# Weight pieces cut from both halves of w_in's rows, and four decay tables made before the Silu table is loaded

## The chip, the cores and the metric

One core of one Trainium2 chip runs the whole kernel as one program. The metric is the device time in microseconds: three runs of the kernel before gave 219.44, 220.36 and 220.79 us, so the median is 220.36 us. Lower is better.

## The reference

A decaying linear attention is followed by a two-layer network with a Silu between the layers. Inputs are float32: q, k and v are (4 batches, 8 heads, 768 positions, 64), lam has one decay rate a head, w_in is 512 x 2048 and w_out is 2048 x 512. The attention goes over blocks of positions with a running 64 x 64 state per head:

```
intra = (q_b @ k_b^T * lam**(i-j) for i >= j) @ v_b
inter = (q_b * lam**(i+1)) @ state
out_b = intra + inter
state = lam**block * state + (k_b * lam**(block-1-j))^T @ v_b
...
x = attention, heads side by side: 3072 tokens x 512
h = x @ w_in                      # 3072 x 2048
out = (h * sigmoid(h)) @ w_out    # 3072 x 512
```

The sum over the 2048 hidden columns in the last line may be taken in any order, as long as column f of w_in meets row f of w_out.

## The kernel before

The 3072 tokens are cut into 24 blocks (units, `u`) of 128 positions, 6 for each batch. For each unit q and k are scaled by powers of lam, turned, multiplied into scores, masked, multiplied with v, and joined with the state from the unit before; the result, turned, is `xt` in bfloat16. Units are joined in groups of one or two. For a group, `first_product` multiplies `xt` with the 16 hidden chunks of 128 columns of `w_in_bf` (L871) and applies Silu on ScalarE (L880), and `second_product` multiplies these with the 16 row chunks of `w_out_bf` (L899). All matmuls are in bfloat16.

The program is written out by a small planner: `Plan.run` keeps a list of operations with costs, dependencies, priorities and buffer rings, walks through time as it estimates it, and so fixes one order of instructions for every engine. Each engine then runs its own order, and waits for other engines by semaphores. Where the planner sees TensorE idle early on, it puts in matmuls on zeros (`warm_ps`, L977).

All input transfers are issued by SyncE in one order (`order`): q, k and v of units 0 and 1, q, k, v of unit 2, then pieces 0 and 1 of w_in, k and v of unit 3, pieces 2 to 5 of w_in, q, k and v of unit 4, pieces 6 and 7, and later units and the eight pieces of w_out. A piece of either weight is 512 KB of float32. It lands in one of 6 slots `wst` of the tile `stage`, in the layout (128 partitions, 2, 512), and one copy on VectorE (L261) casts it into `w_in_bf` or `w_out_bf`.

Piece j of w_in has `m, a = divmod(j, 2)`: rows 256 a to 256 a + 255 and columns 512 m to 512 m + 511. A partition's share is two runs of 2 KB, from two rows that lie 128 rows apart; a row of w_in is 8 KB long. Two pieces with one m feed the same four hidden chunks, so the first product of chunks 4 m to 4 m + 3 waits for pieces 2 m and 2 m + 1. Piece j of w_out is 256 rows of 2 KB that lie one behind the other.

The transfers use eight completion semaphores in turn: each transfer that SyncE issues waits until the one eight before it in the queue has landed.

ScalarE needs a function table for Ln and Exp, and another for Silu; plain copies run with either. The table for Ln and Exp is loaded at L158, `table` (L858) loads the Silu table after the first `xt`. The helper `tables` (L652) makes `lam_bwd_h`, the decay rates of a unit's halves, in four small Exp instructions (L657), and the plan has it not before 20 us. `lam_bwd_h` is first read much later, by the units from 15 on (`attention_by_halves`, L694). Since the Exps stand behind the Silu table, the program loads the Exp table again ahead of them, and the Silu table again ahead of the first Silu (L880).

Of the kernel before, what the change touches and what calls it, by code (L numbers as in the profile page):

```python
# [9 lines left out]
AF = mybir.ActivationFunctionType  # L10
# [90 lines left out]
def kernel(  # L101
# [10 lines left out]
    nc = tc.nc  # L112
# [10 lines left out]
    KO = DFF // 128  # L123
# [12 lines left out]
    plan = Plan()  # L136
# [9 lines left out]
    def sb(o, name, shape, dtype, tag=None):  # L146
        return work.tile(shape, dtype, tag=tag or name, bufs=BUFS[tag or name], name=name)

    def bank(o, name, shape, dtype):
# [5 lines left out]
        out=lam_sb,  # L155
        in_=bass.AP(tensor=lam.tensor, offset=lam.offset, ap=[[0, 128]] + list(lam.ap)),
# [17 lines left out]
        out=ident, in_=ident, compare_op=AL.not_equal, fill=1.0,  # L174
# [6 lines left out]
        out=mask, in_=mask, compare_op=AL.is_ge, fill=0.0,  # L181
# [24 lines left out]
    for hh in range(2):  # L206
        r = slice(64 * hh, 64 * hh + 64)
# [13 lines left out]
    for hh in range(2):  # L221
        r = slice(64 * hh, 64 * hh + 64)
# [4 lines left out]
    lam_bwd_h = const.tile([128, NP, 2], F32)  # L227
    w_in_bf = const.tile([128, KI, DFF], BF16)
    w_out_bf = const.tile([128, KO, DM], BF16)
    w_in_r = moe_w_in.rearrange("(ko p) f -> p ko f", p=128)  # L230
    w_out_r = moe_w_out.rearrange("(ko p) f -> p ko f", p=128)


# [14 lines left out]
    def pace(u):  # L248

        return 0.0 if u < 8 else 57.0 + 6.0 * (u - 8)  # L250
# [35 lines left out]
    for n, (kind, j) in enumerate(order):  # L286
        if kind in "KV":
            u, p = j

            def fn(o, kind=kind, u=u, p=p):  # L290
                b, blk = divmod(u, NB)
                if p == 0:
                    val[kind, u] = regs[o["slots"]["reg"]]
                for hh in range(2):
                    nc.sync.dma_start(
                        out=val[kind, u][64 * hh:64 * hh + 64, p],
                        in_=dict(K=k, V=v)[kind][b, 2 * p + hh, blk * BLK:(blk + NL) * BLK, :].rearrange(
                            "(c s) d -> s c d", c=2 * NL))
            own = load.get((kind, (u, 0)))
            load[kind, j] = prev = plan.op({"SP": 1.1}, [prev], fn, n, alloc=["reg"] if p == 0 else [], at=pace(u) - 18.0)  # L300
            load[kind, j]["own"] = own or load[kind, j]
            continue
        tag = {"k": "kf", "v": "vf", "q": "kf" if j in plain else "qf", "i": "wst", "o": "wst"}[kind]
        us = {"kf": 1.19, "vf": 1.15, "qf": 1.8, "wst": 1.36}[tag]
        if tag == "wst" and order[n - 1][0] not in "io":
            us += 1.7
        elif tag != "wst" and order[n - 1][0] in "io":
            us -= 1.0

        if kind in "kvq" and j > 9:  # L310
            us = 0.75 * us

        def fn(o, kind=kind, j=j, tag=tag):
            if kind in "io":
                t = wst[o["slots"]["wst"]]
            else:
                b, blk = divmod(j, NB)
                sl = slice(blk * BLK, (blk + 1) * BLK)
            if kind in "kvq" and tag != "qf":
                t = sb(o, kind + "f", [128, H, 64], F32, tag)  # L320
                src = dict(k=k, v=v, q=q)[kind]
                nc.sync.dma_start(out=t, in_=src[b, :, sl, :].rearrange("h s d -> s h d"))  # L322
            elif kind == "q":
                t = sb(o, "qf", [128, H, 128], F32)
                nc.sync.dma_start(
                    out=t, in_=q[b, :, blk * BLK:(blk + 2) * BLK, :].rearrange("h (p t) d -> p h (t d)", t=2))
            elif kind == "i":
                m, a = divmod(j, 2)
                nc.sync.dma_start(out=t, in_=w_in_r[:, 2 * a:2 * a + 2, m * 512:(m + 1) * 512])  # L329
            else:  # L330
                nc.sync.dma_start(out=t, in_=w_out_r[:, 2 * j:2 * j + 2, :])
            val[kind + "f", j] = t


        o = plan.op({"SP": us}, [prev], fn, n, alloc=[tag],
                    at=pace(j) - (7.0 if j < 9 else 9.0) if kind in "kvq" else 0.0)
        o["tag"] = tag
        load[kind, j] = prev = o
    at = {key: n for n, key in enumerate(order)}
# [3 lines left out]
    for kind, w, n in (("i", w_in_bf, 8), ("o", w_out_bf, 8)):  # L343
        for j in range(n):
            def fn(o, kind=kind, j=j):
                t = val[kind + "f", j]
                m, a = divmod(j, 2)
                dst = (w_in_bf[:, 2 * a:2 * a + 2, m * 512:(m + 1) * 512] if kind == "i"
                       else w_out_bf[:, 2 * j:2 * j + 2, :])
                copy(o, dst, t)  # L350
            l = load[kind, j]
            cast[kind, j] = plan.op({"DVE": 0.8, "ACT": 1.2}, [l], fn, at[kind, j], frees=[(l, "wst")])
# [4 lines left out]
    O = {}  # L357
# [292 lines left out]

        O["vz", u] = (vc, oo, dd)

    def tables(o):
        for hh in range(2):
            r = slice(64 * hh, 64 * hh + 64)
            for c in range(2):
                nc.scalar.activation(lam_bwd_h[r, :, c], log_lam[r, hh::2], AF.Exp, scale=neg_h[r, c:c + 1])  # L657
    made = plan.op({"ACT": 1.2}, [], tables, 0, at=20.0)

    def attention_by_halves(u):  # L660

        b, blk = divmod(u, NB)
        pr = at["v", u]
        first, last = blk == 0, blk == NB - 1
        lq = load["q", u]
        home = u - (u - XH) % NL
        lk, lv = ([load[kind, (home, p)] for p in range(NP)] for kind in "KV")
        own_k, own_v = lk[0], lv[0]
        late = [plan.op({"NONE": 0.0}, [lq] + lk + lv, lambda o: None, 0, after=2.0, at=pace(u))]
# [3 lines left out]
        def cleared(name, ring, deps):  # L673

            def fn(o):
                val[name, u] = ring[o["slots"][name]]
                (nc.vector if o["eng"] == "DVE" else nc.gpsimd).memset(  # L677
                    val[name, u][:, 0:2 * NP] if name == "kp" else val[name, u], 0.0)
            return plan.op({"POOL": 0.95, "DVE": 0.49}, deps + [O.get(("own", name))], fn, pr, alloc=[name])
# [6 lines left out]
        kz = [cleared("kp", kp_all, late)] if new else []  # L686
        k_own = kz[:1]
        for hh in range(2):
            def fn(o, hh=hh):
                r = slice(64 * hh, 64 * hh + 64)  # L690
                if hh == 0 and not new:
                    val["kp", u] = kp_all[o["slots"]["kp"]]
                t = val["kp", u][:, 0:2 * NP].rearrange("p (a b) (e d) -> p a b e d", b=2, e=2)
                nc.vector.tensor_tensor(  # L694
                    t[r, :, :, hh, :], val["K", home][r, :, cs],
                    lam_bwd_h[r][:, :, :, None].to_broadcast([64, NP, 2, 64]), op=AL.mult)
            kz.append(plan.op({"DVE": 0.7}, [lq, made] + lk + late + kz[-1:], fn, pr,
                              alloc=["kp"] if hh == 0 and not new else [], frees=[(own_k, "reg")] if hh and done else []))
            k_own = k_own or kz[:1]
        k_own[0]["deps"] += [O["own", "kp"]] if ("own", "kp") in O and not new else []  # L700
# [144 lines left out]
    for u in range(NU):  # L845
        n = len(plan.ops)
        (attention if u < XH else attention_by_halves)(u)
        if u >= 8:

            for o in plan.ops[n:]:  # L850
                if "PE" in o["engines"]:
                    o["after"] = 0.8
# [2 lines left out]


    G = {}
    table = plan.op({"ACT": 1.3}, [O["xt", 0]], lambda o: nc.scalar.preload_act_table(AF.Silu), 11)  # L858

    def first_product(g):  # L860
        us = groups[g]
# [151 lines left out]
```

## Time and profile before

| what | value |
|---|---|
| median of three runs | 220.36 us |
| the profiled execution, its own time | 221.07 us |
| its span, first to last instruction | 219.4 us |
| TensorE (PE) matmuls busy | 209.7 us, 96% |
| VectorE (DVE) busy | 122.1 us, 56% |
| ScalarE (ACT) busy | 111.3 us, 51% |
| GpSimd (POOL) busy | 71.7 us, 33% |
| share of the 16 DMA engines taken by SyncE's queue (q1) | 66.6%, 33.37 MB |
| matmuls on zeros (L977) | 8.0 us in 24 instructions |
| first product, L871 | 92.5 us in 896 matmuls |
| second product, L899 | 85.1 us in 368 matmuls |
| w_in transfers, issue to landing, median | 6.9 us for 512 KB |
| w_out transfers, issue to landing, median | 7.3 us for 512 KB |

The span is the time between the first and last instruction of the profiled execution. The 1.67 us between span and that execution's time lie outside the instructions. Busy matmul time is overlapped in the records, so 96% does not say that TensorE works at its peak; where it waits is read from the timeline of its instructions. The granted TensorE clock was 0.997 of full speed.

### The profile page before, as it was taken

The numbers are of one execution on the slowest core, as the hardware profiler recorded it, in microseconds if no ns is written. First come the engines' busy times: TensorE is split into PE (matmuls) and PEld (weight loads), VectorE is DVE, ScalarE is ACT, GpSimd is POOL, SyncE is SP. The second block draws the span as 40 slices with busy tenths as digits, with TensorE's granted clock in tenths as the row PEclk, the third lists the DMA queues.
The fourth block names the chain that finished last, engine by engine and source line by source line (L and its number), as shares of the span: only waits on it lengthen the run. The fifth ranks groups of instructions, "written<-read, shape, count | busy, mean of one in ns | idle before, by whom it ended". The sixth has DMA issues, their size and how long they took to land.

```text
span 219.4 us, 4993 instructions
## 1 busy us (share of the span) xinstructions
PE 209.7 (96%) x2032; PEld 150.2 (68%) x2032; DVE 122.1 (56%) x197; ACT 111.3 (51%) x197; POOL 71.7 (33%) x106
## 2 busy tenths in 40 slices
PE   4989799999999999999999999999999999999994
PEld 1756588998774557955965599758759896854453
DVE  6776566688636786535979468089676221012121
ACT  5598677995473224731953177826617663620000
POOL 8664303036004520321723373248636710000000
PEclk9999999999999999999999999999999999999998
DMA  5998999899999989999983998775985300101212
GB/s 125 240 287 234 271 240 295 208 341 409 234 245 202 314 213 208 165 192 192 228 207 96 229 225 167 156 192 150 209 193 123 71 3 0 51 33 62 96 51 96
DMA packets 104214, 39.78 MB, mean 181 GB/s; under 512 B 93696, under 2 KB 97152, under 8 KB 104192
## 3 DMA queue, kind: packets, MB, share of 16 engines
q1 hardware_dynamic: 100496, 33.37, 66.6%
q10 hardware_dynamic: 3696, 6.10, 8.0%
q8 instruction: 16, 0.26, 0.5%
q14 instruction: 6, 0.05, 0.1%
HBM read 27.27 MB, written 6.29 MB: 153 GB/s over the span
## 4 chain that ended last, share of the span: by engine, by line
PE 79%; SPq 9%; DMA 8%; DVE 1%; issue 1%; POOL 0%; ACT 0%
PE o_ps L899 34%; PE h_ps L871 34%; DMA stage<-in_moe_w_in_dram 6%; SPq L322 4%; SPq L329 4%; DMA xt<-x_sb 2%; PE st_ps L512 2%; PE o_ps L939 2%; PE x_ps L550 1%; PE x_ps L832 1%; PE x_ps L831 1%; PE st_ps L743 1%; PE d_ps L612 1%; DVE w_in_bf L261 1%; PE d_ps L768 1%
## 5 line engine op out<-in xcount | busy, mean ns | idle before, releaser
L871 PE MATMUL h_ps<-xt,w_in_bf 128*128 128x256 bf16 (+1 forms) x896 | 92.5, 257 | 1.0 <-DMA xt<-x_sb 0.4
L899 PE MATMUL o_ps<-w_out_bf,g 128*128 128x512 bf16 x368 | 85.1, 379 | 0.0
L871 PEld LDWEIGHTS <-w_in_bf 128*128 128x128 bf16 x896 | 75.0, 98 | 9.8 <-DVE w_in_bf L261 1.3
L880 ACT ACTIVATE g<-h_ps 128x512 bf16<-128x512 f32 x96 | 56.1, 596 | 27.7 <-PE h_ps L871 26.6
L264 POOL TENSOR_TENSOR Xz<-y,lam_blk 64x256 bf16<-64x256 f32 x40 | 33.3, 831 | 83.9 <-DVE y L628 51.9
L899 PEld LDWEIGHTS <-g 128*128 128x128 bf16 x368 | 34.5, 98 | 35.3
L261 DVE COPY o_sb<-o_ps 128x512 f32<-128x512 f32 (+2 forms) x25 | 16.6, 665 | 40.5 <-PE o_ps L899 38.0
L259 ACT ACTIVATE xt<-x_ps 128x512 bf16<-128x512 f32 x19 | 11.3, 594 | 28.9 <-PE x_ps L554 16.9
L521 DVE TENSOR_TENSOR st_sb<-st_ps,mask 128x512 bf16<-128x512 f32 x30 | 19.8, 686 | 6.2 <-PE st_ps L512 5.7
L264 POOL TENSOR_TENSOR Xf<-y,lam_blk 128x256 f32<-128x256 f32 x18 | 16.2, 898 | 1.4
L261 POOL CAST Xz<-y 64x256 bf16<-64x256 f32 x18 | 9.9, 550 | 18.6 <-PE x_ps L831 9.9
L694 DVE TENSOR_TENSOR kp<-stage,lam_bwd_h 64x512 bf16<-64x512 f32 x18 | 14.3, 795 | 0.9 <-DMA kTz<-kp 0.6
L749 DVE TENSOR_TENSOR st_sb<-st_ps,mask_h 128x512 bf16<-128x512 f32 x9 | 6.2, 688 | 14.2 <-PE st_ps L743 14.2
L512 PE MATMUL st_ps<-qT,kTz 128*128 128x128 bf16 x120 | 10.9, 225 | 1.3 <-ACT kTz L259 0.8
L259 ACT ACTIVATE o_sb<-o_ps 128x128 f32<-128x128 f32 x1 | 0.3, 278 | 23.1 <-DVE o_sb L261 23.1
L512 PEld LDWEIGHTS <-kTz 128*128 128x128 bf16 x120 | 8.4, 101 | 4.5 <-ACT kTz L259 1.3
L628 DVE TENSOR_TENSOR y<-d_ps,Xf 64x256 f32<-64x256 f32 (+1 forms) x17 | 7.2, 421 | 5.4 <-PE d_ps L612 3.8
L259 ACT ACTIVATE vz<-stage 64x512 bf16<-64x512 f32 x15 | 9.4, 626 | 1.1 <-DVE vz L677 0.9
L261 DVE CAST w_in_bf<-stage 128x1024 bf16<-128x1024 f32 x8 | 6.1, 759 | 6.7 <-DMA stage<-in_moe_w_in_dram 6.7
L259 ACT ACTIVATE kTz<-tr_ps 64x512 bf16<-64x512 bf16 (+1 forms) x11 | 8.2, 746 | 2.3 <-PE tr_ps L464 2.2
L977 PE MATMUL warm_ps<-zeros 128*128 128x512 bf16 x24 | 8.0, 452 | 1.3 <-DVE pos L166 1.3
L704 DVE TENSOR_TENSOR kp<-qf,lam_fwd 128x512 bf16<-128x512 f32 x9 | 6.9, 768 | 3.5 <-DMA qf<-in_q_dram 3.3
(91 smaller groups left out, 193.3 us busy)
## 6 DMA issues: line engine op xcount, KB each, us to landing
qf<-in_q_dram SPq DMA_DIRECT2D x18, 256.0 KB, 4.1
out_dram<-o_sb ACTq DMA_DIRECT2D x17, 256.0 KB, 2.4
stage<-in_moe_w_in_dram SPq DMA_DIRECT2D x8, 512.0 KB, 6.9
stage<-in_moe_w_out_dram SPq DMA_DIRECT2D x8, 512.0 KB, 7.3
kf<-in_k_dram SPq DMA_DIRECT2D x15, 256.0 KB, 5.5
vf<-in_v_dram SPq DMA_DIRECT2D x15, 256.0 KB, 5.1
stage<-in_k_dram SPq DMA_DIRECT2D x24, 96.0 KB, 3.0
stage<-in_v_dram SPq DMA_DIRECT2D x24, 96.0 KB, 2.8
```

The source lines that it names most:

```text
L259: nc.scalar.activation(dst, src, AF.Copy)
L261: (nc.vector if o["eng"] == "DVE" else nc.gpsimd).tensor_copy(dst, src)
L264: (nc.vector if o["eng"] == "DVE" else nc.gpsimd).tensor_tensor(dst, a, b, op=op)
L322: nc.sync.dma_start(out=t, in_=src[b, :, sl, :].rearrange("h s d -> s h d"))
L329: nc.sync.dma_start(out=t, in_=w_in_r[:, 2 * a:2 * a + 2, m * 512:(m + 1) * 512])
L512: nc.tensor.matmul(val["st", u, half][:, i, :], lhsT=val["kTz", u][:, h // 2, h % 2, :], rhs=qT(h // 2), start=True, stop=True)
L521: nc.vector.tensor_tensor(val["st_sb", u, half], val["st", u, half], m[:, None, :].to_broadcast([128, 4, BLK]), op=AL.mult)
L694: nc.vector.tensor_tensor(t[r, :, :, hh, :], val["K", home][r, :, cs], lam_bwd_h[r][:, :, :, None].to_broadcast([64, NP, 2, 64]), op=AL.mult)
L871: nc.tensor.matmul(t[:, j, :], lhsT=w_in_bf[:, ko, (m * per + j) * 128:(m * per + j + 1) * 128], rhs=xts[g][:, :, ko, :] if turned(us[0]) ...
L880: nc.scalar.activation(t, val["h", g, m], AF.Silu)
L899: nc.tensor.matmul(val["o", u], lhsT=val["g", g, ko][:, i * BLK:(i + 1) * BLK], rhs=w_out_bf[:, ko, :], start=(ko == 0), stop=(ko == KO - 1))
L977: nc.tensor.matmul(t, lhsT=zeros[:, 0:128], rhs=zeros, start=True, stop=True)
```

## The change

Three edits go together.

1. A row of w_in is seen as two halves (e) of 1024 columns. Piece j now takes columns 256 m to 256 m + 255 of either half, for the same 256 rows. The piece is still 512 KB and lands in the same slot, but is issued as two transfers, one for each 128 rows; a partition's share of one transfer is two runs of 1 KB that lie 4 KB apart. Hidden chunks 4 m and 4 m + 1 now come from the first half, and chunks 4 m + 2 and 4 m + 3 from the second.
2. Piece j of w_out takes the rows that match: from row chunk 8 (j mod 2) + 2 (j div 2). It is still 256 rows in one transfer with runs of 2 KB.
3. The four Exps for `lam_bwd_h` become four operations with a priority and an earliest planned time of 6.5 us, and `table` depends on them, so they stand ahead of the Silu table on ScalarE.

```diff
-    w_in_r = moe_w_in.rearrange("(ko p) f -> p ko f", p=128)
+    w_in_r = moe_w_in.rearrange("(ko p) (e f) -> p ko e f", p=128, e=2)
...
                 m, a = divmod(j, 2)
-                nc.sync.dma_start(out=t, in_=w_in_r[:, 2 * a:2 * a + 2, m * 512:(m + 1) * 512])
+                for kk in range(2):
+                    nc.sync.dma_start(
+                        out=t[:, kk].rearrange("p (e f) -> p e f", e=2),
+                        in_=w_in_r[:, 2 * a + kk, :, m * 256:(m + 1) * 256])
             else:
-                nc.sync.dma_start(out=t, in_=w_out_r[:, 2 * j:2 * j + 2, :])
+
+                r = KO // 2 * (j % 2) + 2 * (j // 2)
+                nc.sync.dma_start(out=t, in_=w_out_r[:, r:r + 2, :])
...
-    def tables(o):
-        for hh in range(2):
-            r = slice(64 * hh, 64 * hh + 64)
-            for c in range(2):
+    made = []
+    for hh in range(2):
+        for c in range(2):
+            def fn(o, hh=hh, c=c):
+                r = slice(64 * hh, 64 * hh + 64)
                 nc.scalar.activation(lam_bwd_h[r, :, c], log_lam[r, hh::2], AF.Exp, scale=neg_h[r, c:c + 1])
-    made = plan.op({"ACT": 1.2}, [], tables, 0, at=20.0)
+            made.append(plan.op({"ACT": 0.3}, [], fn, 10.5, at=6.5))
...
-            kz.append(plan.op({"DVE": 0.7}, [lq, made] + lk + late + kz[-1:], fn, pr,
+            kz.append(plan.op({"DVE": 0.7}, [lq] + made + lk + late + kz[-1:], fn, pr,
...
-    table = plan.op({"ACT": 1.3}, [O["xt", 0]], lambda o: nc.scalar.preload_act_table(AF.Silu), 11)
+    table = plan.op({"ACT": 1.3}, [O["xt", 0]] + made, lambda o: nc.scalar.preload_act_table(AF.Silu), 11)
```

In the resulting program the order of the other engines moves little. SyncE issues the same transfers in the same order, with sixteen for w_in in place of eight. ScalarE has the four Exps two by two on either side of the first `y` copy, only one load of the Silu table, and, further on, the copy `vz` of unit 3 ahead of the copy `xt` of unit 2, where they stood the other way round. TensorE has the state product of unit 3 (L608) ahead of the second part of the first product of group 0, and VectorE the addition `y` that follows from it (L628) ahead of the cast of piece 2. GpSimd's order is the same.

## Prediction

> **What bounds the kernel now.** The 40 slices of the page come first. PE is busy in tenths 9 from the eighth slice (38 us) on, and the slices before it are mixed while the DMA engines are full.
>
> ```profile
> PE   4989799999999999999999999999999999999994
> DMA  5998999899999989999983998775985300101212
> ```
>
> So the end is where PE's packed stretch starts, plus its work. What can move the end is whatever holds PE before it is packed. The sums by stretch put the place between 23.5 and 26.4 us (columns: PE, PEld, DVE, ACT, POOL busy, granted clock, DMA share, GB/s): PE is busy 1.65 of 2.90 us there and 4.92 of 5.00 in the next stretch, at full granted clock.
>
> ```profile
> 23.50:26.40 2.90, 1.65 (x16) 0.83 (x14) 1.17 (x2) 1.93 (x4) 2.07 (x3) 1.00 0.90 247
> 26.40:31.40 5.00, 4.92 (x58) 4.27 (x59) 3.21 (x6) 2.99 (x5) 0.00 (x0) 1.00 0.99 276
> ```
>
> The timelines of PE, DVE and ACT name the two waits in it.
>
> ```profile
> 24.50 0.62 PE L512 MATMUL st_ps<-qT,kTz 128*128 128x128 bf16 x8 [0.85 <-ACT kTz L259]
> ...
> 25.61 0.38 PE L871 MATMUL h_ps<-xt,w_in_bf 128*128 128x256 bf16 x2
> 26.33 1.70 PE L871 MATMUL h_ps<-xt,w_in_bf 128*128 128x256 bf16 x14 [0.35 <-DVE w_in_bf L261]
> ```
> ```profile
> 22.30 0.69 DVE L261 CAST w_in_bf<-stage 128x1024 bf16<-128x1024 f32 x1 [1.42 <-DMA stage<-in_moe_w_in_dram]
> ...
> 25.23 1.05 DVE L261 CAST w_in_bf<-stage 128x1024 bf16<-128x1024 f32 x1 [1.90 <-DMA stage<-in_moe_w_in_dram]
> ...
> 27.89 0.69 DVE L261 CAST w_in_bf<-stage 128x1024 bf16<-128x1024 f32 x1 [0.41 <-DMA stage<-in_moe_w_in_dram]
> 29.14 0.69 DVE L261 CAST w_in_bf<-stage 128x1024 bf16<-128x1024 f32 x1 [0.56 <-DMA stage<-in_moe_w_in_dram]
> ```
> ```profile
> 17.62 1.28 ACT L657 ACT_TABLE_LOAD   x1
> 18.91 0.99 ACT L657 ACTIVATE lam_bwd_h<-log_lam,neg_h 64x4 f32<-64x4 f32 x4
> 20.37 0.60 ACT L259 ACTIVATE xt<-x_ps 128x512 bf16<-128x512 f32 x1 [0.46 <-PE x_ps L554]
> 20.99 0.63 ACT L259 ACTIVATE vz<-vf 128x512 bf16<-128x512 f32 x1
> 21.64 1.28 ACT L880 ACT_TABLE_LOAD   x1
> 22.93 0.60 ACT L880 ACTIVATE g<-h_ps 128x512 bf16<-128x512 f32 x1
> 23.43 1.02 ACT L259 ACTIVATE kTz<-tr_ps 128x1024 bf16<-128x1024 bf16 x1
> ```
>
> First PE waits for ACT, whose `kTz` of unit 3 stands behind a table load; then for the cast of piece 3, which starts as the piece lands, at 25.23. The second wait ends last. Pieces 2 to 5 land at 22.30, 25.23, 27.89 and 29.14, and after 26.33 PE's only waits are some 0.4 us for the cast of piece 5, 0.3 us for ACT and 0.4 us for the cast of piece 7. The front is paced by w_in's transfers.
>
> These are slow for their size. The DMA view of two stretches that hold almost only runs of 2 KB gives the time of a run: 20.5 to 25.5 us (w_in), then 48 to 54 us (w_out).
>
> ```profile
> DMA packets 621, 1.20 MB, mean 240 GB/s; under 512 B 36, under 2 KB 36, under 8 KB 621
> q1 hardware_dynamic: 621, 1.20, 90.3%
> ```
> ```profile
> DMA packets 1247, 2.41 MB, mean 401 GB/s; under 512 B 72, under 2 KB 72, under 8 KB 1247
> q1 hardware_dynamic: 1247, 2.41, 104.0%
> ```
>
> w_in: 0.903 x 16 x 5.0 us = 72.2 us over 585 runs, 123 ns each. w_out: 1.040 x 16 x 6.0 = 99.8 us over 1175, 85 ns. A clean piece is 16 runs an engine, 1.36 us. By landings (issue plus time to landing, per transfer), piece 0 follows the transfer before it (14.05) by 3.4 us, piece 1 by 1.3, piece 2 follows v of unit 3 (20.55) by 1.7, then 2.9, 2.7 and 1.25. Over 1.36 that is an excess of 2.0, 0, 0.35, 1.6, 1.3 and 0: 4.0 us up to piece 3, 5.2 up to piece 5.
>
> **The change, part by part.**
>
> *Runs of 1 KB.* Each engine moves 32 runs for a piece in place of 16. The trace has no 1 KB read. The nearest rows: 1 KB stores at the end (215.7 to 216.25 us: 68.2% of 16 x 0.55 us for 128 runs and 16 small ones, 46 ns), the 512 B reads of q (37.8 to 38.5 us: 106.7% of 16 x 0.70 us for 443, 27 ns), and the clean 2 KB runs. By the bytes of the 2 KB run a piece costs 1.36 us, by the stores 1.47, by the 512 B reads 1.73. I take the stores: +0.11 a piece, +0.45 at piece 3 and +0.67 at piece 5. Ends: 0 and +2.2 at piece 5.
>
> *The excess.* Other reads show none (256 B from 6 to 9 us: 101.3% of 16 x 3.0 us for 2732, 18 ns; 512 B and w_out as above), and these step through memory in 256 B, 512 B and 2 KB, where w_in takes 2 KB of every 8 KB. The new piece takes 1 KB of every 4 KB. Ends: all of it goes (-5.2 at piece 5), or it is a price per run, and twice the runs double it (+5.2). The nearest row is w_in's own, with the same 8 KB rows under the same engines, so I keep most of it and let a fifth go: -0.8 at piece 3, -1.0 at piece 5. With the first term: -0.35 at both.
>
> The Trainium skill ("DMA: Bandwidth & Descriptors", Latency and other measured facts) has a full rate at a row pitch of 512 KiB and about half at 4 MiB, which another 4 KiB in the pitch restores. Its table doesn't reach down to 8 KB; read as "4 KiB apart is another channel" it would take all the excess away (the sum would then be that of the first rival). No trace here shows such a pitch yet.
>
> *Eight more issues on SP.* A w_in issue takes 0.42 to 0.47 us where the queue has room, so a piece costs SP 0.9 us for 1.36 us of transfer. When SP has issued piece 5 (21.0 us), pieces 2 to 5 are not yet landed; that queue hides the 0.45 us more for each piece. Without that cover pieces 2 and 3 would be 0.9 us later. Behind these issues stand q, k, v of unit 4; k and v already block SP for 2.2 and 4.8 us behind a full queue. The new waits on the transfer eight before are met: q of unit 4 waits for the first half of piece 2, which lands near 21.5, k and v for halves up to piece 3, and they only queue behind piece 5 (29.1). ACT's queue issues one transfer, of 4 KB at 0.8 us, in this stage. Cost 0, with 0 and +0.9 as ends.
>
> *Exps before the Silu table.* ACT loses two loads of 1.28 us, and the four Exps (0.99 us) leave 18.91. Their new places are before and after the first `y` copy (8.57), where ACT sits idle 0.48 and 1.24 us; `neg_h` is ready on GpSimd at 7.3. Without that cover, `y` is 0.1 to 1.0 us later. What this frees: `vz` of unit 3 can go when its v lands (20.55), `xt` ends at 21.8, the first Silu at 22.4, and `kTz` at 23.4 in place of 24.45. PE's scores at 24.50 come 1.0 us earlier. But next in PE's order is the first product that waits for piece 3's cast, so the stall moves there. Worth 0 as long as piece 3 lands at 25; ends 0 and -1.0. The new order adds one wait: `vz` stands ahead of `xt`, so v of unit 3, if late by over 0.8 us, holds `xt` and PE's product at 22.59. All of these come before the wait for piece 3, which would be as late.
>
> *Orders of PE and DVE; w_out; loads read later.* The state product and `y` change places with work beside them that lasts 0.9 and 0.7 us, before the same wait. w_out's runs stay 2 KB. Nothing: 0.
>
> *Sum.* PE gets piece 3 and 5 earlier by 0.35 us and all behind moves with it. The profiled execution would go from 221.07 to 220.72, its span from 219.4 to 219.05. It ran 0.71 us above the median of 220.36; against this the forecast is 220.0.
>
> **The rivals.**
>
> *The excess goes (faster).* For it: w_out's clean rows. Against: pieces 1 and 5 show no excess with the same access as 0 and 4, so the address alone does not make it. Piece 3 would land 3.5 us earlier, at 21.7. Then ACT sets the place: scores at 23.5, zeros to 24.0, product done at 25.75 in place of 27.87: 2.1 us, and the wait for piece 5 goes too (0.4). 217.9. The Trainium skill's rule on pitches, named above, would give the same.
>
> *A price per run (slower).* If a slow run waits for something that each read pays once, 32 reads pay twice. For it: excess sits on some runs in full while others are clean; nothing in the trace has 1 KB reads against it. Place: piece 3 lands 4.45 us later and PE stands still before its first product; piece 5, 5.9 us later, adds to it. From +2.2 us at piece 5 on, it decides. 225.9.
>
> *Runs of 1 KB at the price of 512 B runs (slower).* +0.37 a piece, excess unchanged: +2.2 at piece 5, and +0.4 from pieces 6 and 7 (0.74, less the 0.37 us that piece 7 lies landed before its cast at 36.40): 223.0. Against: the 1 KB stores.
>
> *Transfers that pay a fixed time each (slower).* The last store, 64 KB alone in its queue, takes 1.6 us to land, of which its bytes at 401 GB/s are 0.16. If that 1.4 us were paid in turn, six more transfers up to piece 5 would cost 8.6 us, 229. The trace speaks against it: k and v of unit 3, each 256 KB, land 0.9 us apart. The Trainium skill ("DMA: Bandwidth & Descriptors", Anatomy of one DMA) fits 2.0 us plus bytes over 436 GB/s to one transfer, an estimate of 12 us more if taken in turn; with landings 0.9 us apart the trace disagrees with such a sum.
>
> *The transfers are hidden anyway.* Then ACT's 1.0 us could show: 219.4. It falls in the band of the forecast.
>
> **How the numbers follow.** Within 1% (218.2 to 222.6) is about what a measurement of this kernel cannot tell from no change. The forecast with its neighbours has 0.55; the excess gone, or most of it, 0.18; a price per run 0.14; 1 KB at the small runs' price 0.10; fixed times 0.03. The slower ones make 0.27. The likeliest case's own range is 218.6 to 221.6. The range for 8 in 10 takes in the case of no excess, 217.6, and on the other side the dear 1 KB runs (223.0) with 0.6 us of SP's 0.9, 223.6; it leaves out most of the price per run and the fixed times, some 0.17.
>
> **What would show it.** Right: casts of pieces 3 and 5 start within 1 us of 25.2 and 29.1, PE's product behind piece 3 within 1 us of 26.3, `kTz` on ACT ends near 23.4 with the wait then on DVE's cast alone, and w_in runs at about 46 ns clean in the DMA view. Wrong: piece 3 landing before 23.7 (runs at 46 ns throughout) or after 27 (runs above 70 ns); or SP issues of w_in that end after the queue is empty.

## The result and the profile after

| | runs | median | lowest to highest |
|---|---|---|---|
| before | 18 | 219.61 us | 219.12 to 221.03 |
| changed | 18 | 221.53 us | 220.47 to 223.63 |

The ratio changed to before is 1.0083 with a 95% interval of 1.0062 to 1.0103: slower by 0.8%, where 0.2% faster was forecast. The runs were made on several chips, each time with the kernel before measured beside them, so ratios compare better than the times of two runs. The profiled execution of the changed kernel took 222.47 us, 0.94 us above the median; its span was 220.52 us. So 1.95 us lie outside the span, against 1.70 before (span 219.37 us; 1.67 comes of the rounded span).

The slices of the page look like those of before. TensorE is at 9 from the ninth slice on; the eighth (38.6 to 44.1 us) has a 7 where it had a 9:

```profile
PE   4988998799999999999999999999999999999994
DMA  5998999799999898979975989775995300101212
```

The table by stretches (PE, PEld, DVE, ACT, POOL busy, granted clock, DMA share, GB/s) shows where the front loses. PE is short by 0.5 us in the third row, by 0.5 in the fifth and by 1.6 in the last, in which the DMA engines are busy only 0.65 of the time:

```profile
18.00:21.00 3.00, 2.89 (x30) 1.85 (x27) 2.58 (x4) 0.00 (x0) 1.25 (x2) 1.00 0.77 197
21.00:24.00 3.00, 2.76 (x43) 2.55 (x44) 1.10 (x2) 2.82 (x5) 1.11 (x1) 1.00 0.97 279
24.00:29.00 5.00, 4.50 (x56) 3.65 (x54) 3.15 (x5) 2.59 (x6) 1.94 (x3) 1.00 1.05 319
29.00:36.00 7.00, 6.79 (x103) 6.28 (x103) 3.98 (x8) 5.88 (x11) 0.42 (x1) 1.00 0.95 249
36.00:40.00 4.00, 3.52 (x48) 3.08 (x46) 2.65 (x4) 2.44 (x6) 1.36 (x2) 1.00 1.04 257
40.00:44.00 4.00, 2.37 (x41) 2.03 (x38) 1.97 (x4) 1.83 (x4) 0.00 (x0) 1.00 0.65 148
```

The timeline of PE names the waits. The first line is the scores of unit 3, which had waited 0.85 us for ACT; now they wait for nothing and come at 23.86 in place of 24.50. The product behind piece 3 comes at 25.57 (26.33 before). Then two waits over 0.3 us remain: for the cast of piece 7, and, new, 1.43 us for `qs` of unit 6.

```profile
23.86 0.61 PE L518 MATMUL st_ps<-qT,kTz 128*128 128x128 bf16 x8
...
25.57 1.70 PE L878 MATMUL h_ps<-xt,w_in_bf 128*128 128x256 bf16 x14 [0.23 <-DVE w_in_bf L261]
...
36.91 1.70 PE L878 MATMUL h_ps<-xt,w_in_bf 128*128 128x256 bf16 x14 [0.48 <-DVE w_in_bf L261]
...
42.72 0.40 PE L395 MATMUL tr_ps<-ident,qs 128*128 128x128 bf16 x4 [1.43 <-DVE qs L383]
```

VectorE's timeline says what `qs` waited for: q of unit 6 landed at 41.94.

```profile
24.82 0.69 DVE L261 CAST w_in_bf<-stage 128x1024 bf16<-128x1024 f32 x1 [1.32 <-DMA stage<-in_moe_w_in_dram]
...
28.34 0.69 DVE L261 CAST w_in_bf<-stage 128x1024 bf16<-128x1024 f32 x1 [1.03 <-DMA stage<-in_moe_w_in_dram]
...
41.97 1.29 DVE L383 TENSOR_TENSOR qs<-qf,lam_fwd 128x512 bf16<-128x512 f32 x2 [3.19 <-DMA qf<-in_q_dram]
```

ScalarE does what the prediction says: one table load in the front, the Exps in its idle time, `kTz` from 22.67.

```profile
8.17 0.49 ACT L664 ACTIVATE lam_bwd_h<-log_lam,neg_h 64x4 f32<-64x4 f32 x2
...
9.04 0.48 ACT L664 ACTIVATE lam_bwd_h<-log_lam,neg_h 64x4 f32<-64x4 f32 x2
...
22.67 1.03 ACT L259 ACTIVATE kTz<-tr_ps 128x1024 bf16<-128x1024 bf16 x1
```

**The first profile of before was a late one.** A second profile of the kernel before (220.01 us) lacks the wait for piece 3's cast. Piece 3 landed at 22.70, not 25.20, q of unit 6 at 36.66, not 39.80. Its only wait of PE over 0.3 us in the front is this one, for ScalarE:

```profile
24.36 0.62 PE L512 MATMUL st_ps<-qT,kTz 128*128 128x128 bf16 x8 [0.85 <-ACT kTz L259]
```

The first profile's 221.07 us lies at the upper end of the 18 runs (221.03). Six landings, in us, with the start of PE's weight load 400 (those of zeros not counted), from which the rest of the span takes 176.3 to 177.2 us in all four:

| profile | piece 1 | piece 3 | piece 5 | piece 7 | v, unit 5 | q, unit 6 | load 400 |
|---|---|---|---|---|---|---|---|
| before, first | 18.77 | 25.20 | 29.12 | 36.03 | 37.88 | 39.80 | 42.15 |
| before, second | 16.87 | 22.70 | 25.64 | 33.18 | 34.98 | 36.66 | 41.24 |
| changed, first | 18.18 | 24.72 | 28.24 | 36.00 | 37.86 | 41.94 | 43.72 |
| changed, second | 18.05 | 25.07 | 28.04 | 36.07 | 37.93 | 39.90 | 42.46 |

Against the first profile of before, the changed kernel's pieces are early, as forecast. Against the second, pieces 3 to 7 are 2.0 to 2.9 us late. In the second profile of the changed kernel PE does not wait for q of unit 6; it waits for the casts of pieces 3 and 7:

```profile
26.48 1.70 PE L878 MATMUL h_ps<-xt,w_in_bf 128*128 128x256 bf16 x14 [0.87 <-DVE w_in_bf L261]
...
37.62 1.70 PE L878 MATMUL h_ps<-xt,w_in_bf 128*128 128x256 bf16 x14 [0.49 <-DVE w_in_bf L261]
```

### The profile page after: what moved, and what is told of

It reads as the page before. It is cut to its first block, busy times and chain, and to the rows that moved or that the text cites. A ratio compares the mean times of both kernels' runs of the same rounds, so it can differ in the third digit from the quotient of the medians.

```text
span 220.5 us, 4986 instructions
## 1 busy us (share of the span) xinstructions
PE 208.6 (95%) x2012; PEld 150.0 (68%) x2032; DVE 123.1 (56%) x197; ACT 108.4 (49%) x195; POOL 72.2 (33%) x106
## 4 chain that ended last, share of the span: by engine, by line
PE 79%; SPq 9%; DMA 8%; DVE 1%; issue 1%; ACT 1%; POOL 0%; DVEq 0%
PE h_ps L878 34%; PE o_ps L906 34%; SPq L322 5%; DMA qf<-in_q_dram 4%; SPq L331 4%; DMA xt<-x_sb 2%; PE st_ps L518 2%; DMA stage<-in_moe_w_in_dram 2%; PE o_ps L946 2%; PE x_ps L556 1%; PE x_ps L838 1%; PE x_ps L839 1%; PE st_ps L750 1%; PE d_ps L618 1%; PE d_ps L775 1%
## 5 line engine op out<-in xcount | busy, mean ns | idle before, releaser
L906 PE MATMUL o_ps<-w_out_bf,g 128*128 128x512 bf16 x351 | 83.0, 379 | 0.8
L264 POOL TENSOR_TENSOR Xz<-y,lam_blk 64x256 bf16<-64x256 f32 x40 | 34.1, 853 | 83.9 <-DVE y L634 49.7
L259 ACT ACTIVATE vz<-vf 128x512 bf16<-128x512 f32 x9 | 5.6, 625 | 8.4 <-DMA vf<-in_v_dram 8.4
L711 DVE TENSOR_TENSOR kp<-qf,lam_fwd 128x512 bf16<-128x512 f32 x9 | 7.6, 845 | 3.8 <-DMA qf<-in_q_dram 3.6
L984 PE MATMUL warm_ps<-zeros 128*128 128x512 bf16 x21 | 7.5, 463 | 1.4 <-DVE pos L166 1.3
```

Of the source, the lines that this page charges most:

```text
L259: nc.scalar.activation(dst, src, AF.Copy)
L264: (nc.vector if o["eng"] == "DVE" else nc.gpsimd).tensor_tensor(dst, a, b, op=op)
L711: nc.vector.tensor_tensor(val["kp", u][:, 2 * NP:].rearrange("p a (e d) -> p (a e) d", e=2), val["qf", u], lam_fwd[:, 0, :, None].to_broad ...
L906: nc.tensor.matmul(val["o", u], lhsT=val["g", g, ko][:, i * BLK:(i + 1) * BLK], rhs=w_out_bf[:, ko, :], start=(ko == 0), stop=(ko == KO - 1))
```

## The experiments

Each text on record states its theories by a letter. In short, S, and in part R of the first runs: the loss comes with the number of transfers; F: q of unit 6 meets an instruction fetch; A: ScalarE's order; D: the first profile was unlike the others. In the later texts R stands for the split rows, I for SyncE's issue time, and B for the DMA engines between transfers. Ratios are to the kernel before, with 95% intervals.

### Which part costs

**The halves and w_out's order, without the Exps** (edits 1 and 2).

> w_in in two transfers a piece from both halves of the rows, w_out in that order; the Exps stay where they were before. Theory F (fetch): TensorE's instructions arrive in 16 KB transfers on one DMA engine, about one for 250 instructions; the changed kernel has the third of them at 38.15 us, ahead of q of unit 6 on that engine, so q of unit 6 lands at 41.9 in place of 39.8 and TensorE stands still for 1.4 us; TensorE gets there early because pieces 3 and 5 of w_in land 0.5 to 0.9 us earlier. Here the pieces land early just the same, so again q of unit 6 lands near 41.9 and the ratio to before is 1.006 to 1.010. Theory R (runs of 1 KB or the second transfer cost DMA time): the same ratio, but with pieces that land later. Theory A (ScalarE's new order is at fault): 1.000.

1.0038 (1.0010 to 1.0066), less than F and R have it. PE has its 0.85 us for `kTz` again, and 0.56 us for piece 7's cast; v of unit 5 landed at 37.76, and q of unit 6 at 40.13, not near 41.9. The halves, as two transfers a piece, cost.

**The Exps alone** (edit 3).

> Only the four Exps move ahead of the Silu table; w_in and w_out are read as before. Theory F: the scores of unit 3 come 1 us earlier, but TensorE then waits for piece 3 at 25.2 as before, so the third fetch comes after 39 us, q of unit 6 lands near 39.8, ratio 0.997 to 1.003. Theory R: 1.000. Theory A: 1.006 to 1.010.

0.9993 (0.9965 to 1.0021), as F and R have it. In its profile (220.76 us) PE was at load 380 at 39.50, 0.63 us ahead of the second profile of before, and gave it back to q of unit 6, which landed at 40.05:

```profile
40.83 0.40 PE L389 MATMUL tr_ps<-ident,qs 128*128 128x128 bf16 x4 [0.66 <-DVE qs L377]
```

So the Exps do move PE forward, but only up to the next late transfer. The two parts alone, +0.38% and -0.07%, do not add up to the +0.83% of the change: together they cost 0.5% more, which is little above the noise of the three.

**Two transfers a piece, with the runs of 2 KB and the columns of before.**

```diff
-                nc.sync.dma_start(out=t, in_=w_in_r[:, 2 * a:2 * a + 2, m * 512:(m + 1) * 512])
+                for kk in range(2):
+                    nc.sync.dma_start(out=t[:, kk], in_=w_in_r[:, 2 * a + kk, m * 512:(m + 1) * 512])
```

> Before, with each piece of w_in issued as two transfers of 256 KB that keep runs of 2 KB; Exps as before. If the second transfer itself costs (part of theory R): pieces 3 and 5 land later than 25.2 and 29.1 and the ratio is 1.005 or more. If the 1 KB run is what costs: 1.000. Theory F: the ratio follows from where the third 16 KB fetch falls: 1.000 if pieces land as before, 1.006 to 1.010 with q of unit 6 near 41.9 if pieces 3 and 5 land 0.5 us or more earlier.

1.0050 (1.0019 to 1.0082), the ratio that the text gives for a price of the second transfer. Its pieces 3 and 5 landed at 23.33 and 27.42: later than in the second profile of before, but not later than 25.2 and 29.1, the times of the late first profile that the text had set. Neither halves nor runs of 1 KB are needed for a loss; doubling the transfers is enough.

**Four transfers of 128 KB a piece**, on the kernel with the halves alone (each half-row block by itself).

> Halves of the rows with the Exps where they were (as e1), but each piece of w_in as four transfers of 128 KB, one run of 1 KB a partition: 16 more transfers than e1, the same runs. Theory R in the form that each transfer costs: another 0.26 us or more outside the span (16 more transfers at 0.27 us for 8 would be 0.54), and pieces 5 and 7 land 1 to 2 us later than with e1, ratio 1.009 to 1.015. If a transfer costs nothing and the run's size does: ratio as e1, 1.004. The bound of eight transfers in flight now holds at two pieces, which can only add to a loss.

1.0163 (1.0113 to 1.0213), with the same 1 KB runs as with two. Its profile has waits for the casts of pieces 3, 5 and 7 of 0.76, 0.44 and 0.88 us, and q of unit 6 at 42.81. The time outside the span did not grow with it (1.70 us). Eight transfers more cost some 0.4 to 0.5% in these runs, 24 more 1.6%.

### Where it reaches PE

**18 small matmuls on zeros in the kernel before** move the instruction stream, and with it TensorE's instruction fetches, which come as 16 KB transfers on the same DMA engines.

```diff
+            for _ in range(18 if a < 6 else 0):
+                nc.tensor.matmul(t[:, 0:1], lhsT=zeros[:, 0:128], rhs=zeros[:, 0:1], start=True, stop=True)
```

> Before, with 18 more matmuls of one column on zeros at about 3.6 us, where TensorE is idle until 5.5: 36 more instructions for TensorE ahead of everything, and nothing else changed. Theory F: the third fetch is due 36 instructions earlier, near 38.3 us in place of 39.4, ahead of q of unit 6, which lands near 41.5; TensorE waits 1 to 1.6 us for it; ratio 1.005 to 1.008. Theories R and A: 1.000.

0.9996 (0.9976 to 1.0016), where F has 1.005 to 1.008. But the third fetch came at 34.31 us, not near 38.3 (37.76 in the second profile of before), and so ahead of q of unit 6, which landed at 37.64, 1.76 us behind v of unit 5. The run shows that the 18 matmuls cost nothing; whether a fetch beside q does, it does not test.

**The changed kernel, with units 6 and 7 computed from q of units 4 and 5**; their own q is transferred and not read.

```diff
-                    qf = val["qf", u]
+                    qf = val["qf", 4 if u == 6 else u]
```

> The changed kernel, but units 6 and 7 are computed from the q of units 4 and 5 (the transfer of q of unit 6 is still issued, its data is not read), so TensorE has no wait for that transfer. If the wait for q of unit 6 is what the change costs (theory F): TensorE goes on at 41.2 us, 1.0 to 2.0 us earlier than in the changed kernel, held next by k of unit 6 at most 0.5 us; ratio to before 0.997 to 1.003 with the 0.27 us that the changed kernel has outside the span. If the loss lies ahead of it or elsewhere (R, A): 1.005 to 1.009.

1.0008 (0.9979 to 1.0037), as F has it, against 1.0083: some 1.6 us come back. So most of the loss goes with this one wait, though not in every execution: in the changed kernel's second profile PE does not wait there, and load 400 is still 1.2 us later than in the second profile of before, behind the waits for pieces 3 and 7.

In the changed kernel's profile that q landed 4.08 us behind v of unit 5; in the second profile of before it was 1.68. The DMA view of 39.5 to 41.5 us shows the engines almost idle, while 61 runs of 512 B (532 packets of q1 less 471 smaller) are still to come. They are nearly a sixteenth of q's 1024, the share of one engine:

```profile
DMA  9999986532210100000000170000001000355455
...
DMA packets 533, 0.16 MB, mean 78 GB/s; under 512 B 471, under 2 KB 532, under 8 KB 532
q1 hardware_dynamic: 532, 0.15, 32.6%
```

In the stretch before, 38 to 39.5 us, lies a fetch of instructions (6.4% of 16 engines x 1.5 us = 1.5 us on one engine):

```profile
q8 instruction: 1, 0.02, 6.4%
```

The reading: that engine fetched instructions for 1.5 us while the others moved q, and q counts as landed when the last share has. That this engine was the same one is inferred from the times, since the records do not name the engine. One run speaks against a rule: in the run with two transfers of 2 KB runs a fetch lay beside the same q (38.07 us, 0.88 us long), which landed at 38.98, only 1.78 us behind v. After a late stream q meets a fetch at 37 to 39 us (in the run of the Exps alone it landed 3.18 us behind v, with a fetch at 37.53; here, with units 6 and 7 not reading it, 3.74 us, fetch at 37.1). In the changed kernel's second profile the fetch came at 39.46, q at 39.90, 1.97 us behind v, and PE did not wait for it: that execution took 220.77 us, 0.76 us below the median of the changed kernel.

**Second profiles**, of the kernel before and of the changed one.

> The kernel before once more, for a second profiled execution. The first took 221.07 us where the median of 35 executions is 219.5. Theory D (the first profile is of an execution with slow transfers, and in most executions piece 3 of w_in lands early enough that ScalarE alone holds the scores at 24.4 us): about 219.5 us, piece 3 lands at 22.4 to 23.5, piece 5 at 26 to 27, q of unit 6 before 39, no wait before the first product that reads piece 3, and TensorE's load number 400 (without those of zeros) near 41.2 us. Rival: the first profile is typical: piece 3 at 25, piece 5 at 29, load 400 at 42.1.

> The changed kernel once more, for a second profiled execution. Theory D with F: the span is 218.5 to 219.7 us, q of unit 6 lands at 40.5 to 41.5 and TensorE waits for it 0.5 to 1.2 us; load 400 near 42.5. Theory R (the transfers of w_in cost time): piece 5 lands 1 to 2 us later than in the kernel before's second profile, and piece 7 too. Rival A: no wait for q of unit 6, the loss lies elsewhere.

Both are in the table above. Before came out as D has it. The changed kernel did not as D with F has it (q at 39.90, no wait for it), but as rival A has it, and as R, with more than its 1 to 2 us: pieces 5 and 7 landed 2.4 and 2.9 us later than in the second profile of before.

### How many transfers

**Eight small transfers more in the kernel before**, 64 bytes to each partition behind each piece.

```diff
+                nc.sync.dma_start(out=extra[:, 16 * j:16 * j + 16], in_=w_in_r[:, 0, 16 * j:16 * j + 16])
```

> The kernel before with one more transfer of 64 bytes a partition (8 KB in all) behind each of the 8 pieces of w_in, read by nothing. Theory S (each transfer more costs, by its issue on SyncE and by idle time between transfers, whatever its bytes): piece 3 lands 0.5 to 1 us later than in the second profile of the kernel before (22.70), piece 5 at about 27 instead of 25.64, PE's weight load 400 at about 41.9 instead of 41.2, the time 1.003 to 1.006 of before. Theory R (the loss comes with the split rows or the bytes of the pieces, not with their number): pieces and weight load 400 as in the second profile of before within 0.4 us, the time 0.998 to 1.002.

1.0043 (1.0017 to 1.0069), as S has it. Its profile is of a late execution (222.17 us, median 220.61), with piece 3 at 24.66. But a run of 64 B took 11 ns, so the 8 transfers have 0.7 us of work on every engine, which the text had not counted; by itself the run does not separate bytes from number.

**Two neighbouring pieces as one transfer of 1 MB**, with the Exps ahead and without.

```diff
-                nc.sync.dma_start(out=t, in_=w_in_r[:, 2 * a:2 * a + 2, m * 512:(m + 1) * 512])
+                if a:
+                    s = o["slots"]["wst"] - 1
+                    nc.sync.dma_start(
+                        out=stage[:, 1024 * s:1024 * (s + 2)].rearrange("p (k f) -> p k f", k=4),
+                        in_=w_in_r[:, :, m * 512:(m + 1) * 512])
```

> Exps ahead of the Silu table as in the change, and two neighbouring pieces of w_in as one transfer of 1 MB with runs of 2 KB, so 4 transfers in place of 8. Theory S: fewer issues and fewer boundaries, so the stream to q of unit 6 is about 1 us ahead of the second profile of before (36.66), PE has the 0.85 us that ScalarE's kT took, no wait for q of unit 6: the time 0.995 to 0.998 of before. Theory R: the number of transfers does nothing, the time is that of the run with the Exps alone, 0.998 to 1.002. A loss is open too: a pair counts as landed only when both pieces have, so that PE's product behind piece 2 waits for piece 3's bytes (about 1 us at 22.7): then 1.002 to 1.006.

> Two neighbouring pieces of w_in as one transfer of 1 MB with runs of 2 KB, the Exps where they were. Theory S: transfers land earlier, but PE's products behind pieces 2 and 3 still wait for ScalarE's kT (0.85 us at 24.4 in the second profile of before): 0.997 to 1.001 of before. Theory R: 0.999 to 1.002. Against the run with pairs and Exps this gives what the Exps are worth when the stream is not late.

With the Exps 0.9963 (0.9944 to 0.9982), without 1.0009 (0.9993 to 1.0024). The time is as S has it, but its reason is not: q of unit 6 landed at 36.45 and 36.88, next to no earlier than in the second profile of before. Without the Exps, 4 transfers in place of 8 gain nothing. What the pair shows is the worth of the Exps when the stream is not late: 0.46%, 1.0 us. Without them PE waits 0.85 us for `kTz`, and with them not. With the eight transfers of before, the run of the Exps alone showed 0.07% of it, and its q of unit 6 was late.

**The changed kernel with 8 transfers.** One half of the columns for two neighbouring pieces, 512 KB with the same runs of 1 KB, is one transfer.

```diff
-                for kk in range(2):
-                    nc.sync.dma_start(
-                        out=t[:, kk].rearrange("p (e f) -> p e f", e=2),
-                        in_=w_in_r[:, 2 * a + kk, :, m * 256:(m + 1) * 256])
+                if a:
+                    s = o["slots"]["wst"] - 1
+                    pair = stage[:, 1024 * s:1024 * (s + 2)].rearrange("p (k f) -> p k f", k=4)
+                    for e in range(2):
+                        nc.sync.dma_start(
+                            out=pair[:, :, 256 * e:256 * (e + 1)],
+                            in_=w_in_r[:, :, e, m * 256:(m + 1) * 256])
```

> The changed kernel with the same halves, the same order and the same runs of 1 KB, but each transfer brings one half of the columns for two neighbouring pieces (512 KB), so that w_in takes 8 transfers as before the change, not 16. Theory S (the number of transfers, by their issue on SyncE and the idle time between them): the loss goes, v of unit 5 lands at about 35 to 36 instead of 37.9, PE's weight load 400 starts at 40.3 to 41.3 instead of 42.5 to 43.7, the device time outside the span falls back from 1.95 to 1.72 us, the time is 0.996 to 0.999 of before. Theory R (the halves themselves: runs of 1 KB, two products of columns far apart): the loss of the changed kernel stays, 1.004 to 1.009.

0.9966 (0.9944 to 0.9989): the loss is gone, as S has it, and about what the Exps are worth is left. 1.70 us lie outside the span again. Load 400 starts at 40.26, and PE has no wait over 0.3 us left between 6 and 40 us:

```profile
23.18 0.61 PE L521 MATMUL st_ps<-qT,kTz 128*128 128x128 bf16 x8
...
39.64 0.61 PE L398 MATMUL tr_ps<-ident,qs 128*128 128x128 bf16 x8
```

Its stretches, beside those of the changed kernel, have the DMA engines full where those had 0.77 and 0.65:

```profile
18.00:21.00 3.00, 2.94 (x34) 2.17 (x32) 2.49 (x4) 1.18 (x3) 1.21 (x2) 1.00 1.05 352
...
40.00:44.00 4.00, 4.00 (x76) 4.00 (x73) 2.66 (x6) 3.72 (x8) 0.00 (x0) 1.00 0.92 332
```

The DMA views of w_in's stretch, first the changed kernel from 20.5 to 25.5 us, then this one from 20 to 24 us:

```profile
DMA packets 1492, 1.42 MB, mean 285 GB/s; under 512 B 107, under 2 KB 1492, under 8 KB 1492
q1 hardware_dynamic: 1492, 1.42, 96.7%
```
```profile
DMA packets 1523, 1.44 MB, mean 359 GB/s; under 512 B 47, under 2 KB 1523, under 8 KB 1523
q1 hardware_dynamic: 1523, 1.44, 105.7%
```

The rate is 26% higher. 9 points of it are busier engines (105.7 over 96.7). The rest is faster runs: by their records the runs of 1 KB took 55 ns on average in the first stretch and 48 ns in the second. So this kernel has both less idle time and less of what the prediction called excess, with the same run length and the same rows.

That the transfers are larger does not explain the faster runs. The kernel before has transfers of 512 KB too, and over all of w_in its runs of 2 KB took 108 and 102 ns on average in the two profiles, as long for their bytes as the changed kernel's 54 and 52 ns for 1 KB. In the kernel with 8 transfers it was 48 ns, in the two with 4 transfers 94 and 96 ns for 2 KB. In these three a transfer brings four runs to a partition, in the others two or one. No run separates the two: this kernel differs from the changed one in the shape of its transfers as well as in their number.

### By what a transfer costs

**SyncE held up without a transfer more**: on the kernel with 8 transfers, 20, then 40 additions in one of SyncE's registers behind each of the 8. They were to hold it up for about as long as the issues of the changed kernel's 8 further transfers; what an addition takes, no run shows.

```diff
+                        for i in range(20):
+                            nc.sync.reg_add(late, late, 1)
```

> [...] Theory I (what is lost with 16 transfers is lost because SyncE issues too late): unit 5's v lands about 2 us later than without the additions (34.3), the first product's weight load 400 starts at 41.5 to 43 instead of 40.3, the time is 1.002 to 1.008 of before. Theory B (it is lost between transfers on the DMA engines): landings and weight load 400 as without the additions within 0.5 us, the time 0.995 to 0.999.

> [...] Theory I: about twice the loss of the run with 20, 1.006 to 1.02 of before. Theory B: the transfers of pieces 2 to 5 still queue behind one another as long as SyncE is blocked anyway; 0.995 to 1.001, with a loss beginning only where an issue ends after its predecessor has landed.

0.9933 (0.9908 to 0.9959) and 0.9938 (0.9916 to 0.9960). They decide nothing between I and B: an issue still starts 0.05 us after the one before has ended (17.16 and 17.21 us with 40 additions), so the additions took no time that can be seen; that they were left out because nothing reads the register is inferred. What is left is the kernel with 8 transfers, measured twice more: three times faster than before, by 0.3 to 0.7%.

**Eight more transfers that one partition gets, and eight that all partitions get**, on the same kernel.

```diff
+                        i = 16 * (2 * m + e)
+                        nc.sync.dma_start(out=extra[0:1, i:i + 16], in_=w_in_r[0:1, 0, e, i:i + 16])
```

> The changed kernel with 8 transfers of 512 KB for w_in, and behind each a transfer of 64 bytes to one partition, read by nothing: one run of data, so next to no work for the DMA engines, but SyncE's issue (0.35 to 0.5 us) eight times. Theory I (SyncE's issues make the loss): v of unit 5 lands 1 to 2 us later than without them (33.8 to 34.5), weight load 400 at 41.5 to 43, the time 1.001 to 1.008 of before. Theory B (the loss arises on the DMA engines, where all of them go from one transfer to the next): landings and weight load 400 within 0.5 us of the three runs without them (40.3 to 40.7), the time 0.994 to 0.998.

> The same with 64 bytes to each of the 128 partitions, so that all DMA engines take part in each of the 8 transfers: 0.09 us of work an engine and transfer by the 11 ns of such a run, 0.7 us in all. Theory I: as with the transfers to one partition. Theory B: the loss comes here and not there, weight load 400 at 41 to 42.5, the time 0.999 to 1.006 of before; a hand-over between transfers that costs nothing beyond the runs would give 0.7 us at most, so 0.994 to 0.999.

0.9998 (0.9980 to 1.0015) and 1.0009 (0.9992 to 1.0025). SyncE did take the time for the first kind:

```profile
17.53 0.37 SPq L339 DMA_DIRECT2D extra<-in_moe_w_in_dram  x1
17.94 0.90 SPq L335 DMA_DIRECT2D stage<-in_moe_w_in_dram  x1
18.89 0.36 SPq L339 DMA_DIRECT2D extra<-in_moe_w_in_dram  x1
```

Yet load 400 was at 40.70, within 0.44 us of the three profiles without (40.26, 40.52, 40.70), as B has it; the ratio lies between the two theories. About 0.27 us of its loss lie outside the span (1.97 us there, against 1.70 and 1.71). With all partitions load 400 was at 41.68, 1 us later, of which 0.7 us could be the work of the runs of 64 B. So 8 transfers more with next to no data cost 0.3 to 0.65%, 0.7 to 1.4 us, outside included (the lower end is within the intervals); from the changed kernel to the one with 8 transfers it is 1.2 to 1.5%, 2.6 to 3.3 us. That does not yet clear SyncE: its issues here were shorter (0.37 us) than those of the changed kernel's halves (0.61 us), and the last for piece 5 ended at 20.49 us, not at 23.62. How the price divides between SyncE's issues and the DMA engines stays open, and so does why runs were slower beside more transfers.

## Why the prediction was wrong

*What bounds the kernel.* The reading of the rows was right for that execution, and wrong for the typical one. It ran 0.7 us above the median then known and 1.5 above the median of 18 runs, and the prediction used that only to shift the sum. In the second profile PE waits for ScalarE alone, so "the front is paced by w_in's transfers" held in a late stream, not in general.

*Runs of 1 KB, +0.11 a piece.* Right for a clean run: the median run of 1 KB took 46 ns in every profile that has them, the 46 taken from the stores. Split rows lose nothing by themselves; the rival "1 KB at the price of 512 B runs" is out.

*The excess, a fifth gone.* The two DMA terms together came out nearly right. Over all of w_in the packets kept an engine busy for 13.9 and 13.0 us in the two profiles of before and for 13.7 and 13.2 us in those of the changed kernel, so of the 2.8 us by which piece 7 landed later than in the second profile of before, at most 0.7 us lie in the packets themselves. The excess is neither the address alone (the changed kernel keeps it, the one with 8 transfers, 12.2 us, has nearly lost it, from the same rows) nor a price per run (the same runs). Both rivals built on those are out. The time of the second of them, 225.9, is 5.9 us on the forecast of 220.0, which has 0.35 us of excess taken off already; on the median it would be 226.2.

*Eight more issues on SP, cost 0, ends 0 and +0.9.* This is the step that failed. The price was sought only in SyncE's issue and thought hidden behind the queue. What the runs showed in its place is a price for every further transfer. Where nothing but the number of transfers changed, eight more cost 0.50%, 1.1 us; the halves without the Exps cost 0.38%, 0.8 us; 24 more cost 1.63%, 3.6 us. That is 0.10 to 0.15 us a transfer. In the changed kernel, transfers made late by it also met PE at q of unit 6 and took away what the Exps are worth (1.0 us), so that against the kernel with 8 transfers the whole is 2.6 to 3.3 us; the faster runs of that kernel are in this too.

On SyncE an issue took 0.61 us a half, 1.2 a piece, not 0.9, and piece 2's first was held until 19.04 us (in the two profiles of before until 18.66 and 16.88):

```profile
13.70 0.61 SPq L331 DMA_DIRECT2D stage<-in_moe_w_in_dram  x1
...
15.73 3.31 SPq L331 DMA_DIRECT2D stage<-in_moe_w_in_dram  x1
```

From 19 to 20 us the DMA engines were then busy 0.28 of the time (0.43 and 0.84 before). In the kernel with 8 transfers the four issues of pieces 2 to 5 end at 19.34 instead of 23.62. But the issue time is not all of it: for the halves with runs of 2 KB an issue took 0.43 us, as the prediction has it, and the loss came. The runs with extra transfers do not divide the rest.

The nearest rival is "transfers that pay a fixed time each", given 0.03: a price for each transfer came, but its size (1.4 us each, 229 us) was about ten times too large. The evidence against it, k and v 0.9 us apart, excluded that size and not a smaller one. The fit that the prediction takes from the Trainium skill ("DMA: Bandwidth & Descriptors", Anatomy of one DMA) stands there for transfers that GpSimd issues; these are SyncE's. The Trainium skill ("DMA: Bandwidth & Descriptors", Bandwidth) advises transfers of 1 MiB and more. By this case's runs, 512 KB beat 256 KB, and 1 MB without the Exps (1.0009) was no better than 512 KB.

*Exps before the Silu table, 0, ends 0 and -1.0.* The local times came out (`kTz` ends at 23.70, forecast 23.4). The value is the other end: 1.0 us between the kernels with pairs. Since PE's next wait was thought to be piece 3, it was set at 0; in the changed kernel the late transfers do take it away, so the 0 holds there, for that reason.

*Where the stall goes.* The prediction followed the stream as far as piece 5. What was late next was piece 7's cast (0.48 us) and q of unit 6 (1.43 us), and neither was named. In that execution the second was worth most of the loss; in the second profile of the changed kernel it was 0, and the casts of pieces 3 and 7 (0.87 and 0.49 us) held PE.

*Outside the span.* 0.25 us of the 1.9 us lie there, and the sum had no such term. It came with 16 transfers in w_in's stage, small ones counted (1.91 to 1.98 us outside in all these profiles), and not with 4, 8 or 32 (1.70 to 1.73 us); its cause is open.

The signs of being right that the prediction set (casts of pieces 3 and 5, PE behind piece 3, `kTz`) all came in the changed profile. Set against a late profile, they could not show the loss. One sign of being wrong, an issue of w_in that ends after the queue is empty, nearly came too, in the gap from 19 to 20 us; the first profile of before has such a gap as well.

## What to carry to other kernels

Splitting a transfer is not free because its bytes and its run length stay the same: here eight more transfers cost 0.8 to 1.1 us by themselves, and some 2 us more where they also made a load late that a packed engine waits for and so hid another gain. The same halves in transfers of 512 KB cost nothing. If the profiled execution lies at the upper end of the runs, read a second one before calling a wait the bound. Where a stream of loads feeds a packed engine, follow it to its last reader, since the last transfer that is waited for decides, not the one at the edit.

## What was not expected of the hardware

TensorE's instructions come in 16 KB transfers, some 250 instructions apart (16 of them for 2032 matmuls and as many weight loads), each 0.9 to 2.3 us long. In three profiles with such a transfer beside it or just ahead, q of unit 6, which is spread over all engines, landed 3.2 to 4.1 us behind v of unit 5 in place of some 1.7; in a fourth it landed 1.78 us behind it. That the fetch is the reason is inferred from the times. In the changed kernel's first profile that was the last q that PE waited for. And the same 1 KB runs, 46 ns when clean, took 51 to 54 ns on average in transfers of 128 and 256 KB, and 48 ns in transfers of 512 KB that bring four runs to a partition.
